# Attention with top-32 scores, then two feed-forward layers: the threshold from fours of scores, a stricter hand-over to GpSimd, shared work tiles, a new order of the steps

## The chip, the cores and the metric

One core of one Trainium2 chip. The metric is the device time of one execution in microseconds, the median of several runs.

## The reference

Attention over 4 batches, 8 heads, 576 positions and 64 dimensions, where each row keeps only the scores that reach its 32nd largest; then two feed-forward layers (512 to 2048 to 512) on the 2304 tokens, the first with a rational function between its products, the second with a squared relu.

```python
scores = scale * np.matmul(q, k.transpose(0, 1, 3, 2))
kth = np.partition(scores, -top_k, axis=-1)[..., -top_k:-top_k + 1]     # top_k = 32
scores = np.where(scores >= kth, scores, -1e9)
attn = np.exp(scores - max); attn = attn / (sum + 1e-9)
x = attn @ v                                                             # tokens x 512
h = x @ w_in;  g = P(h) / (Q(h) + 1e-6);  x = g @ w_out                  # P cubic, Q = 1 + |b0||h| + |b1|h2
h = x @ w_in2; x = np.maximum(h, 0) ** 2 @ w_out2
```

## The kernel before

The kernel is written as steps, and a planner written in Python sets the order of all instructions before anything runs.

**The steps.** `load_q`, `load_k` and `load_v` fetch and split operands into two fp16 halves. `attend(t, j)` (line 596) does one pair of heads for one of 18 tiles of 128 tokens: TensorE writes scores to `ps_sx`, ScalarE copies them to `sb`, VectorE finds the threshold, ScalarE takes the exponential to `ex`, VectorE masks it and sums it (`ex<-sb,kth,ex`), ScalarE and GpSimd split it into `ahl` (line 674), and SP issues a transposing DMA to `at`. The product with v (`mix`, line 684) comes three heads later (`LAGA`) and writes `xn`; after the last head the tile is transposed into `xT`. `w_load` fetches one of 32 weight units as 64-bit floats, makes them 32-bit on VectorE in `f4k` (lines 747 to 749) and splits them; 7 stay in SBUF (`wr`), 25 go back to DRAM (`wd`) and are reloaded into the ring `wt`. `consts1` and `consts2` need all units of their layer. The feed-forward works in ten blocks of 1 or 2 tiles; step u of a block computes the hidden product of unit u (`g1`), its function (`rational`, line 881, or `relu2`, line 905), and the output product of unit u - 2 (`g2`).

**The threshold before.** Scores i and i + 288 form a pair. VectorE writes the larger of each pair and the smaller of each, finds the 32 largest of the 288 larger ones (`largest`, line 632: MAX8 four times, MATCH_REPLACE8 three times) and the 8 largest of the smaller ones, and merges the two lists in `kths` and `kth` (lines 658, 659). `more` notes rows in which eight smaller ones would not do; if there is one, the whole kernel runs again with an exact search (line 1031).

**The order.** `at` (line 961) gives each step a place, read between knots of the list `KN`; a step comes no sooner than those it needs. The steps are sorted by place and each operation takes its step's place as its priority. `Plan.emit` then plays the engines with costs: an engine that is free takes the ready operation of the lowest place. `ANY` operations may go to GpSimd or VectorE; VectorE counts as `PEN` later. Instructions that GpSimd and VectorE can't run side by side (`port`: all of GpSimd's, and VectorE's with two inputs in SBUF) take turns in this play. In hardware nothing orders them except line 286: a GpSimd operation waits for the VectorE operation that held the port last, if it held it less than `LATE` = 500 ns earlier in the play:

```python
if e == "Pool" and holder is not None and holder.eng[0] == "DVE" and now < port + LATE:
    o.behind = holder
```

Each tile tag has a ring of `BUFS` places (line 472), given out in the order in which the steps name them. Each engine, and SP's DMA queue with it, runs its instructions in the order so planned.

Of the kernel before, what the change touches and what calls it, by code (L numbers as in the profile page):

```python
# [15 lines left out]
OP = mybir.AluOpType  # L16
# [9 lines left out]

PEN = 1e4

KN = [-1000000, 1000000000, 0, 34900, 89700, 131400, 186900, 217700, 292000, 325300, 345200, 429100,
# [5 lines left out]

LATE = 500.0
BEHIND = mybir.DependencyInfo(mybir.DependencyClass.Sync, mybir.DependencyReason.DATA)
# [19 lines left out]
class View:  # L57
# [42 lines left out]
    def bitcast(self, dt):  # L100
# [3 lines left out]
        return v  # L104

    def ap(self):
        t = self.tile
        if t.real is None:
            key = (t.tag, t.slot)
            if key not in t.pool[1]:  # L110
                name = f"{t.tag}_{t.slot}"
                t.pool[1][key] = t.pool[0].tile(list(t.shape), t.dtype, name=name, tag=name)
            t.real = t.pool[1][key]
        a = t.real
        for what, x in self.steps:
            if what == "get":
                a = a[x]
            elif what == "bitcast":
                a = a.bitcast(x)
            elif what == "pairs":  # L120
# [16 lines left out]
class Op:  # L137
    __slots__ = ("eng", "dur", "nbytes", "calls", "need", "next", "tiles", "prio", "ready", "n", "first", "start", "got", "port", "behind", "last")

# [10 lines left out]
class Plan:  # L150
# [4 lines left out]
    def __init__(self, tc):  # L155
        self.tc, self.ops, self.at, self.cur = tc, [], 0.0, None

# [25 lines left out]
    def _op(self, eng, cost, nbytes):  # L183
# [3 lines left out]
        o.nbytes, o.calls, o.need, o.next, o.tiles, o.prio, o.ready = nbytes, [], 0, {}, {}, self.at, 0.0  # L187
        o.n, o.first, o.port = len(self.ops), [], False
        self.ops.append(o)
# [20 lines left out]
    def emit(self):  # L210
# [19 lines left out]
        while events:  # L230
# [18 lines left out]
            for e in engines:  # L249
# [3 lines left out]
                while ready[e]:  # L253
# [187 lines left out]
def tile_topk_attention_moe_moe(ctx: ExitStack, tc: tile.TileContext, qx, kx, vx, vtx, vraw, wx, ma, mb, out):  # L441
# [25 lines left out]
    def run(exact):  # L467

        plan = Plan(tc)
        E = Engines(nc, plan)  # L470
        plan.at = KN[0] - 1e6
        BUFS = dict(ks=2, kacc=2, kf=2, ksc=2, ki=2, khn=2, kl=5, kd=5, vs=2, vh=5, vts=1, vt=5,
                    qs=1, qh=1, ql=1, qacc=2, qf=2, qsc=2, qi=2, qt=2, sc=2, nsc=2, top=2, w=1, kths=2, kth=2, bias=4, z=4, at=4, zi=5,
                    xn=2, xhl=2, xT=2, f4k=2, wt=6, sq=1, m_r=3, m_f=3, m_q=3, g1h=3, g1l=3, g2h=3, g2l=3,
                    yn2=2, yf=2, ysc=2, yis=4, yhl=1, yT=1, zd=2, zo=1, ps_sx=1, ps_h=2)
# [116 lines left out]
        waiting = []  # L592
        xns, kths_of, scs = {}, {}, {}
        more = new([P, NT, H], BF16, "more")

        def attend(t, j):
# [23 lines left out]
            for b, lo, hi in ps:  # L620

                whole = (b, H // 2 - 1) in kv if j == 0 else scs[t, b] 
                scs[t, b] = whole
                if j == 0 or not whole:
# [19 lines left out]
            else:  # L644

                if j == 0:
                    kths_of[t] = new([P, H, 9], F32, "kths"), new([P, H], F32, "kth")
                kths, kth = kths_of[t]
                h2 = slice(2 * j, 2 * j + 2)
                tb = tbs[pair % len(tbs)]  # L650
                E.tt("DVE", w[:, :, :S // 2], sb2[:, :, :S // 2], sb2[:, :, S // 2:S], OP.max)
                E.tt("DVE", w[:, :, S // 2:], sb2[:, :, :S // 2], sb2[:, :, S // 2:S], OP.min)
                for e in range(2):
                    big, small = w[:, e, :S // 2], w[:, e, S // 2:]
                    largest(top[:, e], big, big, K)
                    E.max8(tb[:, e, 1:], small)

                E.tt("DVE", kths[:, h2], top[:, :, K - 1:K - 10:-1], tb, OP.min)
                E.reduce(kth[:, h2], kths[:, h2], OP.max)
                kth = [kth[:, 2 * j + e:2 * j + e + 1] for e in range(2)]  # L660
                if j == H // 2 - 1:

                    E.tt("DVE", more[:, t], kths[:, :, 8], kths_of[t][1], OP.is_ge)
            z, zi = new([P, 2], F32, "z"), new([P, 2], F32, "zi")
# [46 lines left out]

        sbs, exs, ahls, tbs = [], [], [], []
        for n in range(2):
            tbs.append(new([P, 2, 9], F32, f"tb{n}"))
            E.memset("Pool", tbs[-1][:, :, 0], -NEG)
        for n in range(2):
# [17 lines left out]
        resident, scratch = {}, {}  # L734
        nres = [0]

        def w_load(m, u, io):
# [25 lines left out]
            if keep:  # L763
                wt = new([P, 2, 2, 512], F16, f"wr{nres[0]}")
                nres[0] += 1
            else:
                wt = new([P, 2, 2, 512], F16, "wt")
# [113 lines left out]
        def rational(hp, n, u):  # L881
# [75 lines left out]

        KVA = 4
# [6 lines left out]
        def between(ka, kb, f):  # L965
            return (ka, kb, f, KN[ka] + (KN[kb] - KN[ka]) * f)

        def item(n):
            t = min(max(n, 0) // H, NT - 1)
            return between(2 + t, 3 + t, n / H - t)  # L970

        def moe_at(m, i, k):

            a = 3 + NT + 2 * (m * NB + i)
            return between(a, a + 1, k / (NU + LAG))

        def w_at(m, k):
            a = 3 + NT + 4 * NB + 5 * m
            n = min(k // 4, 3)
            return between(a + n, a + n + 1, k / 4 - n)  # L980

        NK = 3 + NT + 4 * NB + 10
        start, end = (0, 0, 0.0, KN[0]), (1, 1, 0.0, KN[1])
        at(start, load_q, 0)
        at(start, load_k, 0, 0)
        first = (NK, NK, 0.0, KN[NK])
        scale = [at(first, v_scale)]
        seen = {(0, 0): [at(first, load_v, 0, 0, after=scale)]}
        items = []
        for n in range(NT * H):  # L990
            t, h = divmod(n, H)
            need = items[-1:]
            for b, _, _ in parts(t):
                j = h // 2
                if (b, j) not in seen:
                    seen[b, j] = [at(item(n - KVA), f, b, j, after=a) for f, a in ((load_k, ()), (load_v, scale))]
                need += seen[b, j]
            if h == 0 and t > 0:
                need.append(at(item(n - KVA), load_q, t))
            if h % 2 == 0:  # L1000
                items.append(at(item(n), attend, t, h // 2, after=need))
        items.append(at(item(NT * H), mix_rest, after=items[-1:]))
        ready = []
        for m in range(2):
            for k in range(2 * NU):
                ready.append(at(w_at(m, k), w_load, m, k // 2, k % 2))
            ready += scale
            ready = [at(w_at(m, 2 * NU), (consts1, consts2)[m], after=ready)]
            for i, (t0, n) in enumerate(blocks):
                x = min(((t0 + n) * H + LAGA - 1) // 2, NT * H // 2)  # L1010
                last = [items[x]] if m == 0 else [firsts[i]]
                for k, f in enumerate(moe_steps(m, i)):
                    last = [at(moe_at(m, i, k), f, after=last + ready)]
                if m == 0:
                    firsts[i] = last[0]
        for x, n, f in sorted(steps, key=lambda s: s[:2]):
            plan.at = x
            f()
        if not exact:
            plan.at = KN[1]  # L1020
            bad, n, flag = new([P, 1], F32, "bad"), new([P, 512], F32, "ps_h"), new([P, 1], I32, "flag")
# [57 lines left out]
```

## Time and profile before

| | |
|---|---|
| median of 3 runs | 1321.45 us (1319.78 to 1321.8) |
| the profiled execution's own time | 1320.17 us |
| its span, first to last instruction | 1318.4 us |
| mean granted TensorE clock in the span | 0.940 |

The profile is of one execution. Its names are PE (TensorE), PEld (TensorE's weight loads), DVE (VectorE), ACT (ScalarE), POOL (GpSimd) and SP with its DMA queue SPq. Tiles carry the names of the code without their buffer numbers, and L362 is the helper line through which almost every operation of VectorE, ScalarE and GpSimd is recorded, so groups are told apart by tile. "Mean ns" is the duration of one instruction from start to end; neighbours on one engine can overlap, so busy time is less than count times mean.

### The profile page before, as it was taken

The page shows a single profiled execution, that of the slowest core. Times are in us where ns is not written, and L with a number is a line of the kernel's source. Part 1 is how long each engine was busy: PE and PEld are TensorE (multiplying, and loading weights), DVE is VectorE, ACT ScalarE, POOL GpSimd, SP SyncE. Part 2 cuts the span into 40 slices and gives each one's busy share as a digit, 9 for nine tenths or more (in the row PEclk, how much of TensorE's full clock was granted, in tenths as well). Part 3 has the DMA queues.
Part 4 walks back from the last instruction along what each step waited for, and adds up shares of the span by engine and source line. Part 5 has one row for each costly group of instructions (what it writes and reads, how often), then busy time and mean ns, then how long its engine had stood idle before and what let it go on. Part 6 is the DMA issues. An engine that isn't in the chain of part 4 may idle for free. (4 is left out here: it accounts for less than half of the span.)

```text
span 1318.4 us, 25413 instructions
## 1 busy us (share of the span) xinstructions
PE 1045.2 (79%) x8808; PEld 673.3 (51%) x8808; DVE 1129.3 (86%) x3298; ACT 997.3 (76%) x1796; POOL 553.4 (42%) x458
## 2 busy tenths in 40 slices
PE   2123254555789698979996999999999899999998
PEld 1112132333456365646653666656665566666665
DVE  5999989879999999999989899998999999983511
ACT  7866667667878787879987789888887877775543
POOL 2234424234454445445655555654653564330000
PEclk9999995665889998989998999999999999999999
DMA  8977775878579675778886768879777877865854
GB/s 259 288 250 232 224 245 177 252 222 241 161 187 258 178 184 161 198 171 211 222 198 161 186 179 207 235 168 215 193 197 177 197 191 171 206 195 175 251 183 161
DMA packets 299868, 269.18 MB, mean 204 GB/s; under 512 B 236368, under 2 KB 246096, under 8 KB 299728
## 3 DMA queue, kind: packets, MB, share of 16 engines
q1 hardware_dynamic: 299728, 267.45, 75.1%
q8 instruction: 71, 1.16, 0.4%
q14 instruction: 69, 0.57, 0.1%
HBM read 183.50 MB, written 17.83 MB: 153 GB/s over the span
## 5 line engine op out<-in xcount | busy, mean ns | idle before, releaser
L428 PEld LDWEIGHTS <-wt 128*128 128x128 f16 x3120 | 286.4, 101 | 65.2 <-issue 8.8
L362 POOL TENSOR_TENSOR ahl<-ex,ahl 128x576 f16<-128x576 f32 x144 | 182.5, 1282 | 300.0 <-ACT ahl L362 113.7
L362 DVE MAX8 top<-w 128x8 f32<-128x288 f32 x576 | 239.4, 444 | 0.1
L428 PE MATMUL ps_h<-xT,wt 128*128 128x256 f16 (+1 forms) x1680 | 193.4, 273 | 5.5 <-ACT f4k L362 2.1
L362 DVE MATCH_REPLACE8 w<-top,w 128x288 f32<-128x288 f32 x432 | 188.3, 440 | 0.0
L428 PE MATMUL ps_h<-yT,wt 128*128 128x256 f16 (+1 forms) x1440 | 159.0, 263 | 0.0
L428 PE MATMUL ps_sx<-vh,at 128*128 128x64 f16 (+1 forms) x1920 | 88.7, 202 | 81.7 <-DMA at<-ahl 58.9
L428 PEld LDWEIGHTS <-at 128*128 128x128 f16 (+1 forms) x2400 | 96.3, 107 | 111.7 <-DMA at<-ahl 74.5
L428 PE MATMUL ps_y<-wt,g1h 128*128 128x512 f16 x432 | 137.3, 401 | 13.0 <-DMA wt<-wd 9.7
L428 PE MATMUL ps_y<-wt,g2h 128*128 128x512 f16 x432 | 129.0, 380 | 0.0
L362 ACT ACTIVATE ex<-sb,bias,sc 128x576 f32<-128x576 f32 x144 | 119.1, 861 | 10.7 <-POOL ahl L362 7.4
L362 DVE TENSOR_TENSOR w<-sb 128x576 f32<-128x576 f32 x144 | 108.3, 768 | 19.1 <-ACT sb L362 18.8
L362 POOL TENSOR_TENSOR m_f<-m_f,m_q 128x512 f32<-128x512 f32 (+1 forms) x55 | 67.8, 1233 | 133.8 <-ACT m_q L362 63.5
L362 ACT ACTIVATE sb<-ps_sx 128x576 f32<-128x576 f32 x144 | 92.5, 642 | 40.0 <-PE ps_sx L428 39.6
L362 DVE SCALAR_TENSOR_TENSOR ex<-sb,kth,ex 128x577 f32<-128x577 f32 x144 | 119.0, 858 | 1.3 <-ACT sq L362 0.6
L428 PEld LDWEIGHTS <-qt 64*128 64x128 f16 (+3 forms) x640 | 41.2, 100 | 132.6 <-issue 108.0
L428 PE MATMUL ps_sx<-kl,qt 64*128 64x512 f16 (+1 forms) x320 | 74.5, 317 | 40.7 <-ACT xn L362 22.2
L362 ACT ACTIVATE ahl<-ex 128x576 f16<-128x576 f32 x144 | 93.2, 674 | 8.8 <-DVE ex L362 8.6
L362 ACT ACTIVATE xn<-ps_sx,zi 128x64 f32<-128x64 f32 x144 | 44.2, 307 | 72.1 <-PE ps_sx L428 71.4
L362 POOL TENSOR_TENSOR wt<-f4k,wt 128x1024 f16<-128x1024 f32 x25 | 53.2, 2129 | 108.1 <-ACT ahl L362 36.8
L428 PE MATMUL ps_y<-wt,g1l 128*128 128x512 f16 x216 | 86.6, 401 | 7.4 <-POOL g1l L362 7.4
L362 ACT ACTIVATE f4k<-ps_h,cu 128x512 f32<-128x512 f32 (+1 forms) x80 | 50.8, 636 | 48.0 <-PE ps_h L428 48.0
(164 smaller groups left out, 2357.5 us busy)
## 6 DMA issues: line engine op xcount, KB each, us to landing
wt<-wd SPq DMA_DIRECT2D x250, 512.0 KB, 4.1
wt<-in_wx_dram SPq DMA_DIRECT2D x64, 512.0 KB, 5.9
wd<-wt SPq DMA_DIRECT2D x25, 512.0 KB, 3.1
qs<-in_qx_dram SPq DMA_DIRECT2D x18, 256.0 KB, 4.3
ks<-in_kx_dram SPq DMA_DIRECT2D x16, 288.0 KB, 4.2
wt<-in_vraw_dram SPq DMA_DIRECT2D x12, 384.0 KB, 6.2
kd<-khn SPq DMA_DIRECT2D x64, 72.0 KB, 3.1
out_dram<-zo SPq DMA_DIRECT2D x18, 256.0 KB, 2.5
```

Source lines behind the costliest of these rows:

```text
L362: return f(**{k: self.ap(x) for k, x in kw.items()})
L428: self.plan.add("PE", self.cols(out) * passes / 2.4 + 3, lambda e: self.nc.tensor.matmul(self.ap(out), self.ap(lhsT), self.ap(rhs), start= ...
```

## The change

1. The threshold search goes by fours. The larger of each pair are paired once more: `u` holds the 144 largest of fours. The 8 largest of each of three remaining groups (two halves of the smaller ones of the second pairing, 72 scores each, and the 288 smaller ones of the first) are written behind them, and the 32 largest are sought among these 168. `kths`, `kth` and `tb` go; `more` compares each group's 8th with the threshold, now once a pair of heads.
2. GpSimd waits for VectorE's last holder of the port however long ago that was in the play.
3. The rational step's `m_f` and `m_q` become two halves of one `f4k` tile, of which there are 5 instead of 2. Its first two activations change places, and its second and third VectorE operations with them.
4. Every step has a place of its own in a list `PLACES` of 358 numbers, in place of 72 knots; the needs between the first loads are written out; `PEN` is 8457 instead of 10000.

```diff
-PEN = 1e4
-KN = [-1000000, 1000000000, 0, 34900, 89700, 131400, 186900, 217700, 292000, 325300, 345200, 429100,
...
-LATE = 500.0
+PEN = 8457
+PLACES = [-101131, -104946, -1423, 566, -464, -4302, -788, 916, -725, -1069, 1322, 1333, -1127, 780, 1067, 2727, 4109,
...
+          141508, 141328, 141417, 144751, 141347, 138173, 140740]
...
-                        if e == "Pool" and holder is not None and holder.eng[0] == "DVE" and now < port + LATE:
+                        if e == "Pool" and holder is not None and holder.eng[0] == "DVE":
                             o.behind = holder
...
-                    xn=2, xhl=2, xT=2, f4k=2, wt=6, sq=1, m_r=3, m_f=3, m_q=3, g1h=3, g1l=3, g2h=3, g2l=3,
+                    xn=2, xhl=2, xT=2, f4k=5, wt=6, sq=1, m_r=3, g1h=3, g1l=3, g2h=3, g2l=3,
...
-                E.tt("DVE", w[:, :, :S // 2], sb2[:, :, :S // 2], sb2[:, :, S // 2:S], OP.max)
-                E.tt("DVE", w[:, :, S // 2:], sb2[:, :, :S // 2], sb2[:, :, S // 2:S], OP.min)
+                h2, n = slice(2 * j, 2 * j + 2), S // 4
+                u = new([P, 2, n + 24], F32, "u")
+                E.tt("DVE", w[:, :, :2 * n], sb2[:, :, :2 * n], sb2[:, :, 2 * n:S], OP.max)
+                E.tt("DVE", w[:, :, 2 * n:], sb2[:, :, :2 * n], sb2[:, :, 2 * n:S], OP.min)
+                E.tt("DVE", u[:, :, :n], w[:, :, :n], w[:, :, n:2 * n], OP.max)
+                E.tt("DVE", w[:, :, :n], w[:, :, :n], w[:, :, n:2 * n], OP.min)
                 for e in range(2):
-                    big, small = w[:, e, :S // 2], w[:, e, S // 2:]
-                    largest(top[:, e], big, big, K)
-                    E.max8(tb[:, e, 1:], small)
-
-                E.tt("DVE", kths[:, h2], top[:, :, K - 1:K - 10:-1], tb, OP.min)
-                E.reduce(kth[:, h2], kths[:, h2], OP.max)
-                kth = [kth[:, 2 * j + e:2 * j + e + 1] for e in range(2)]
-                if j == H // 2 - 1:
-
-                    E.tt("DVE", more[:, t], kths[:, :, 8], kths_of[t][1], OP.is_ge)
+                    for k, (lo, hi) in enumerate(((0, n // 2), (n // 2, n), (2 * n, 4 * n))):
+                        E.max8(u[:, e, n + 8 * k:n + 8 * k + 8], w[:, e, lo:hi])
+                    largest(top[:, e], u[:, e], w[:, e, :n + 24], K)
+                kth = [top[:, e, K - 1:K] for e in range(2)]
+
+                E.tt("DVE", more[:, t, h2], u[:, :, n + 7::8], top[:, :, K - 1:K].wide(3), OP.is_ge)
...
-            f, q, r, gh, gl = (t(x, F16 if x[0] == "g" else F32) for x in ("m_f", "m_q", "m_r", "g1h", "g1l"))
-
+            fq = new([P, 2, 512], F32, "f4k")
+            f, q = fq[:, 0, :n], fq[:, 1, :n]
+            r, gh, gl = (t(x, F16 if x[0] == "g" else F32) for x in ("m_r", "g1h", "g1l"))
+
+            E.act(f, hp, AF.Identity, scale=k("f_s"), bias=k("f_b"))
             E.act(q, hp, AF.Abs, scale=k("q_s"))
-            E.act(f, hp, AF.Identity, scale=k("f_s"), bias=k("f_b"))
+            E.tt("DVE", f, f, hp, OP.mult)
             E.stt(q, q, k("bd"), hp, OP.add, OP.mult)
-            E.tt("DVE", f, f, hp, OP.mult)
...
-        def at(x, f, *args, after=()):
-            steps.append((max([x[3]] + [steps[k][0] for k in after]), len(steps), lambda: f(*args)))
+        def at(f, *args, after=()):
+            p = 10.0 * PLACES[len(steps)]
+            steps.append((max([p] + [steps[k][0] for k in after]), len(steps), lambda: f(*args)))
             return len(steps) - 1
```

`wide(3)` repeats a column three times as an operand.

## Rows read from the trace of the kernel before

**Rows 1.** Page, part 1: busy us (share of the span) xinstructions, by engine.
```profile
PE 1045.2 (79%) x8808; PEld 673.3 (51%) x8808; DVE 1129.3 (86%) x3298; ACT 997.3 (76%) x1796; POOL 553.4 (42%) x458
```

**Rows 2.** Windows by stage: length, busy us (x) by engine, clock, DMA share, GB/s.
```profile
0.00:300.00 300.00, 112.80 (x806) 72.60 (x806) 260.85 (x774) 209.99 (x350) 101.28 (x82) 0.87 0.78 236
300.00:1150.00 850.00, 770.31 (x6692) 490.77 (x6693) 798.23 (x2388) 693.10 (x1270) 437.00 (x365) 0.95 0.78 195
1150.00:1318.40 168.40, 162.12 (x1312) 109.92 (x1310) 70.18 (x137) 94.20 (x177) 15.13 (x13) 0.99 0.61 192
```

**Rows 3.** Critical chain, some of its pieces: start us, us, what.
```profile
1114.65 5.55 DMA xT<-xhl
...
1147.58 2.62 PE ps_h L428 x24
...
1309.11 3.27 PE ps_y L428 x15
```

**Rows 4.** Timeline at 640 us, VectorE, then GpSimd: start us, us, instruction.
```profile
640.33 1.86 DVE L362 SCALAR_TENSOR_TENSOR ex<-sb,kth,ex 128x577 f32<-128x577 f32 x1
...
640.30 1.28 POOL L362 TENSOR_TENSOR g1h<-m_f,m_r 128x512 f16<-128x512 f32 x1
```

**Rows 5.** By tile, VectorE, whole span: ns min/median/max, first and last start us.
```profile
L362 DVE TENSOR_TENSOR w<-sb x144: 726/747/1482, 19.0 to 1137.9; 128x576 f32<-128x576 f32 x144
...
L362 DVE SCALAR_TENSOR_TENSOR ex<-sb,kth,ex x144: 800/812/1859, 28.2 to 1147.6; 128x577 f32<-128x577 f32 x144
...
L362 DVE TENSOR_TENSOR kths<-top,tb x72: 158/170/1251, 27.3 to 1145.3; 128x18 f32<-128x18 f32 x72
...
L362 DVE SCALAR_TENSOR_TENSOR m_q<-m_q,cc,g1h x80: 471/742/1752, 186.5 to 1247.2; 128x512 f32<-128x512 f32 x64, 128x256 f32<-128x256 f32 x16
```

**Rows 6.** Groups on VectorE, 300 to 1150 us: busy us, mean ns, idle before.
```profile
L362 DVE MAX8 top<-w 128x8 f32<-128x288 f32 x479 | 198.6, 444 | 0.0
...
L362 DVE SCALAR_TENSOR_TENSOR ex<-sb,kth,ex 128x577 f32<-128x577 f32 x120 | 98.8, 858 | 0.2
L362 DVE TENSOR_TENSOR w<-sb 128x576 f32<-128x576 f32 x118 | 89.3, 772 | 15.8 <-ACT sb L362 15.5
...
L362 DVE SCALAR_TENSOR_TENSOR m_q<-m_q,cc,g1h 128x512 f32<-128x512 f32 x56 | 45.4, 811 | 1.5 <-POOL g1h L362 1.3
...
L362 DVE TENSOR_TENSOR kths<-top,tb 128x18 f32<-128x18 f32 x60 | 17.4, 290 | 0.2
...
L362 DVE TENSOR_TENSOR g1l<-m_f,m_r 128x512 f16<-128x512 f32 x14 | 9.5, 678 | 0.0
...
L362 DVE TENSOR_TENSOR g1h<-m_f,m_r 128x512 f16<-128x512 f32 x8 | 5.6, 701 | 2.5 <-ACT m_r L362 1.3 <-ACT m_f L362 1.1
```

**Rows 7.** Timeline inside one search, VectorE, then GpSimd.
```profile
613.98 0.81 DVE L362 MAX8 top<-w 128x8 f32<-128x288 f32 x2
614.71 0.08 DVE L362 MATCH_VALUE_LOAD w<-top,w 128x8 f32 x1
614.77 0.45 DVE L362 MATCH_REPLACE8 w<-top,w 128x288 f32<-128x288 f32 x1
...
613.05 2.53 POOL L362 TENSOR_TENSOR ahl<-ex,ahl 128x576 f16<-128x576 f32 x2 [3.31 <-ACT ahl L362]
```

**Rows 8.** Groups on VectorE over the whole span, by shape.
```profile
L362 DVE TENSOR_TENSOR m_f<-m_f,ps_h 128x512 f32<-128x512 f32 x64 | 43.3, 677 | 3.5 <-ACT m_f L362 3.5
...
L362 DVE TENSOR_TENSOR m_f<-m_f,ps_h 128x256 f32<-128x256 f32 x16 | 6.6, 413 | 0.2 <-ACT m_f L362 0.2
```

**Rows 9.** Windows: the 100 us from 600 us on, columns as in rows 2.
```profile
600.00:700.00 100.00, 96.32 (x816) 63.07 (x814) 94.44 (x277) 90.43 (x168) 60.21 (x53) 0.98 0.84 218
```

**Rows 10.** Waits: TensorE 300 to 1150 us, SP's queue whole span: us, times, longest.
```profile
PE ps_sx L428 <- DMA at<-ahl: 32.1, 21, 5.6
...
PE ps_y L428 <- POOL g1l L362: 9.7, 5, 6.1
...
SPq L436 <- POOL ahl L362: 169.1, 64, 9.7
```

More of the change, by code (lines that the diff above doesn't have):

```diff
@@ L104, in bitcast, with wide @@
         return v
+    def wide(self, n):
+        return self._with(self.shape[:-1] + (n,), self.box, ("wide", n))
     def ap(self):
@@ L119, in ap @@
                 a = a.bitcast(x)
+            elif what == "wide":
+                a = bass.AP(a.tensor, a.offset, list(a.ap)[:-1] + [[0, x]])
             elif what == "pairs":
@@ L137 @@
 class Op:
-    __slots__ = ("eng", "dur", "nbytes", "calls", "need", "next", "tiles", "prio", "ready", "n", "first", "start", "got", "port", "behind", "last")
+    __slots__ = ("eng", "dur", "nbytes", "calls", "need", "next", "tiles", "prio", "ready", "n", "first", "start", "got", "port", "behind", "last", "step")
 LATENCY = {"ACT": (145.0, {"PE": 163.0, "Pool": 170.0}), "DVE": (128.0, {"Pool": 155.0}), "PE": (197.0, {"PE": 0.0}),
@@ L155, in __init__ @@
     def __init__(self, tc):
-        self.tc, self.ops, self.at, self.cur = tc, [], 0.0, None
+        self.tc, self.ops, self.at, self.cur, self.step = tc, [], 0.0, None, -1
     def tile(self, pool, shape, dtype, tag, bufs=1):
@@ L187, in _op @@
         o.nbytes, o.calls, o.need, o.next, o.tiles, o.prio, o.ready = nbytes, [], 0, {}, {}, self.at, 0.0
-        o.n, o.first, o.port = len(self.ops), [], False
+        o.n, o.first, o.port, o.step = len(self.ops), [], False, self.step
         self.ops.append(o)
@@ L470, in run @@
         E = Engines(nc, plan)
-        plan.at = KN[0] - 1e6
+        plan.at = FIRST - 1e6
         BUFS = dict(ks=2, kacc=2, kf=2, ksc=2, ki=2, khn=2, kl=5, kd=5, vs=2, vh=5, vts=1, vt=5,
-                    qs=1, qh=1, ql=1, qacc=2, qf=2, qsc=2, qi=2, qt=2, sc=2, nsc=2, top=2, w=1, kths=2, kth=2, bias=4, z=4, at=4, zi=5,
-                    xn=2, xhl=2, xT=2, f4k=2, wt=6, sq=1, m_r=3, m_f=3, m_q=3, g1h=3, g1l=3, g2h=3, g2l=3,
+                    qs=1, qh=1, ql=1, qacc=2, qf=2, qsc=2, qi=2, qt=2, sc=2, nsc=2, top=2, w=1, u=1, bias=4, z=4, at=4, zi=5,
+                    xn=2, xhl=2, xT=2, f4k=5, wt=6, sq=1, m_r=3, g1h=3, g1l=3, g2h=3, g2l=3,
                     yn2=2, yf=2, ysc=2, yis=4, yhl=1, yT=1, zd=2, zo=1, ps_sx=1, ps_h=2)
@@ L592, in run @@
         waiting = []
-        xns, kths_of, scs = {}, {}, {}
-        more = new([P, NT, H], BF16, "more")
+        xns, scs = {}, {}
+        more = new([P, NT, H, 3], BF16, "more")
         def attend(t, j):
@@ L620, in attend @@
             for b, lo, hi in ps:
-                whole = (b, H // 2 - 1) in kv if j == 0 else scs[t, b]
-                scs[t, b] = whole
+                whole = t > b * S // P
                 if j == 0 or not whole:
@@ L644, in attend @@
             else:
[L646 to L650, printed above, removed]
-                E.tt("DVE", w[:, :, :S // 2], sb2[:, :, :S // 2], sb2[:, :, S // 2:S], OP.max)
-                E.tt("DVE", w[:, :, S // 2:], sb2[:, :, :S // 2], sb2[:, :, S // 2:S], OP.min)
-                for e in range(2):
-                    big, small = w[:, e, :S // 2], w[:, e, S // 2:]
-                    largest(top[:, e], big, big, K)
-                    E.max8(tb[:, e, 1:], small)
-                E.tt("DVE", kths[:, h2], top[:, :, K - 1:K - 10:-1], tb, OP.min)
-                E.reduce(kth[:, h2], kths[:, h2], OP.max)
-                kth = [kth[:, 2 * j + e:2 * j + e + 1] for e in range(2)]
-                if j == H // 2 - 1:
-                    E.tt("DVE", more[:, t], kths[:, :, 8], kths_of[t][1], OP.is_ge)
+                h2, n = slice(2 * j, 2 * j + 2), S // 4
[4 more added lines that the diff above has]
+                E.tt("DVE", w[:, :, :n], w[:, :, :n], w[:, :, n:2 * n], OP.min)
+                for e in range(2):
+                    for k, (lo, hi) in enumerate(((0, n // 2), (n // 2, n), (2 * n, 4 * n))):
[3 more added lines that the diff above has]
+                E.tt("DVE", more[:, t, h2], u[:, :, n + 7::8], top[:, :, K - 1:K].wide(3), OP.is_ge)
             z, zi = new([P, 2], F32, "z"), new([P, 2], F32, "zi")
@@ L709, in mix @@
                 E.dma_transpose(xT[i][:, :, k * P:(k + 1) * P], xhl.flat(), 2 * P * 1024)
[L712 to L715, printed above, removed]
+        sbs, exs, ahls = [], [], []
         for n in range(2):
@@ L734, in run @@
         resident, scratch = {}, {}
-        nres = [0]
         def w_load(m, u, io):
@@ L763, in w_load @@
             if keep:
-                wt = new([P, 2, 2, 512], F16, f"wr{nres[0]}")
-                nres[0] += 1
+                wt = new([P, 2, 2, 512], F16, f"wr{(n * RESIDENT) // (4 * NU)}")
             else:
@@ L955, in moe_steps @@
             return [lambda u=u: step(u) for u in range(NU + LAG)]
-        KVA = 4
         steps, firsts = [], {}
-        def at(x, f, *args, after=()):
-            steps.append((max([x[3]] + [steps[k][0] for k in after]), len(steps), lambda: f(*args)))
+        def at(f, *args, after=()):
+            p = 10.0 * PLACES[len(steps)]
+            steps.append((max([p] + [steps[k][0] for k in after]), len(steps), lambda: f(*args)))
             return len(steps) - 1
[L965 to L988, printed above, removed]
+        q0 = at(load_q, 0)
+        k0 = at(load_k, 0, 0)
+        scale = [at(v_scale)]
+        seen = {(0, 0): [k0, at(load_v, 0, 0, after=[k0] + scale)]}
         items = []
@@ L995, in run @@
                 if (b, j) not in seen:
-                    seen[b, j] = [at(item(n - KVA), f, b, j, after=a) for f, a in ((load_k, ()), (load_v, scale))]
+                    seen[b, j] = [at(load_k, b, j, after=seen[b, 0][:1] if j else ())]
+                    seen[b, j].append(at(load_v, b, j, after=seen[b, j] + scale))
                 need += seen[b, j]
+            if t == 0:
+                need = need + [q0]
             if h == 0 and t > 0:
-                need.append(at(item(n - KVA), load_q, t))
+                need.append(at(load_q, t))
             if h % 2 == 0:
-                items.append(at(item(n), attend, t, h // 2, after=need))
-        items.append(at(item(NT * H), mix_rest, after=items[-1:]))
+                items.append(at(attend, t, h // 2, after=need))
+        items.append(at(mix_rest, after=items[-1:]))
         ready = []
@@ L1005, in run @@
             for k in range(2 * NU):
-                ready.append(at(w_at(m, k), w_load, m, k // 2, k % 2))
+                ready.append(at(w_load, m, k // 2, k % 2))
             ready += scale
-            ready = [at(w_at(m, 2 * NU), (consts1, consts2)[m], after=ready)]
+            ready = [at((consts1, consts2)[m], after=ready)]
             for i, (t0, n) in enumerate(blocks):
@@ L1012, in run @@
                 for k, f in enumerate(moe_steps(m, i)):
-                    last = [at(moe_at(m, i, k), f, after=last + ready)]
+                    last = [at(f, after=last + ready)]
                 if m == 0:
@@ L1016, in run @@
         for x, n, f in sorted(steps, key=lambda s: s[:2]):
-            plan.at = x
+            plan.at, plan.step = x, n
             f()
+        plan.step = -2
         if not exact:
-            plan.at = KN[1]
+            plan.at = LAST
             bad, n, flag = new([P, 1], F32, "bad"), new([P, 512], F32, "ps_h"), new([P, 1], I32, "flag")
```

1 line of the change is left out of this document (added), and 27 rows, old and new, of tables (KN, PLACES).

## The prediction, made before the changed kernel ran

> **What bounds the kernel now.** I read the engine totals first [rows 1]. VectorE leads with 86% of the span, but that is an average over unlike stages, so the second view cuts the span into three [rows 2]. Up to 300 us the weights, q, k and v come in and TensorE works 113 us of 300. From 300 to 1150 us VectorE is busy 798.23 of 850 us (94%) and TensorE 770.31 (91%). From 1150 us on TensorE is busy 162 of 168 us and VectorE 70. The chain of waits begins, as far as it was followed, at 1114.65 us with the transposed tokens of a feed-forward block, and ends in output products at 1309.11 us [rows 3]. The reader is to see a relay: VectorE sets when the last attention tile is through, then TensorE works off two blocks of the first layer and three of the second, which by the sorted places all come behind that tile or hang on the block ahead of it. So a microsecond saved on VectorE before 1150 us moves the tail forward by a microsecond, if TensorE and the port can follow; saved later it is worth nothing.
>
> A second bound hides behind VectorE. The diff's "port" is the thing that GpSimd and two-input VectorE instructions hold in turns. In [rows 4] GpSimd ran g1h from 640.30 us for 1.28 us, and VectorE's masking product, started 0.03 us later, took 1.86 us where its median is 0.812 [rows 5]: it stood until GpSimd was done. Over 300 to 1150 us GpSimd holds the port 437.0 us [rows 2]; on VectorE the masking product holds it 98.8, the pairwise max and min 89.3, the product with g1h 45.4, the compare for kths 17.4 and three smaller groups 21.9 [rows 6]. Together 710 of 850 us: the port is taken 84% of the time.
>
> **The threshold search: the working time.** Rows give durations, but VectorE's instructions overlap: two MAX8 in a row last 0.81 us, not 2 x 0.444 [rows 6], and starts in a run are about 0.08 us closer than the durations [rows 7]. So a MAX8 over 288 advances the engine by 0.365 us, a MATCH_REPLACE8 with its value load by 0.36 + 0.065, a max or min over 576, by its median of 0.747 [rows 5], by 0.665. No row has the new sizes. The 512 and 256 wide forms of one multiply give 677 - 413 ns for 256 elements, 1.03 ns each [rows 8]; with this slope, a MAX8 over 168 advances by 0.24, over 72 by 0.14, a MATCH_REPLACE8 over 168 by 0.235 (+0.065), a max or min over 288 by 0.365.
> Before, per pair of heads: 2 x 0.665, then per head 5 x 0.365 + 3 x 0.425 = 3.10, then 0.19 for kths, kth and the share of the flag compare: 7.72 us. After: 2 x 0.665 + 2 x 0.365, then per head 2 x 0.14 + 0.365 + 4 x 0.24 + 3 x 0.30 = 2.51, then 0.08 for the flag compare: 7.16 us. The saving is 0.56 us a pair, 40 us over 72 pairs: 34 us of it in the 60 pairs from 300 to 1150 us, 6 in the 12 before. Bounds: if nothing overlapped and every instruction cost its whole duration, 9.38 against 9.19, or 14 us in all (five instructions more per pair eat the rest); if an instruction had no fixed part, 816 elements less a pair, 61 us. I take 40, since the starts in the rows are what the engine does.
>
> The Trainium skill has a rule against this change: "VectorE: DVE Perf Modes", section "The DRAIN you can't avoid", says that the next instruction does not start until the pipeline is empty, so small ones pay in full. By that rule the saving would be the 14 us above. The trace differs here: the starts 613.98, 614.71 and 614.77 leave no such gap.
>
> **The search: the port.** MAX8 and MATCH_REPLACE8 have one input, and GpSimd runs beside them: two GpSimd operations from 613.05 to 615.58 us lie inside one search [rows 7]. The change takes 85 us of that cover away (6.20 less 5.02 us a pair) and adds two two-input operations: 0.73 + 0.08 us a pair, less kths. From 300 to 1150 us the port then needs 710 + 49 - 17 = 741 us, VectorE 798 - 34 = 764. Three operations of a first-layer step and one of a second-layer step may run on either engine; one moved to VectorE frees the port by 1.28 [rows 4] less 0.60 us (g1l's 678 ns [rows 6] less the overlap) and costs VectorE 0.60. If the port can be filled to 92% (100 us from 600 on come near: GpSimd 60.2 there, plus the middle's 32 of VectorE [rows 9]) nothing need move and the stretch takes 764/0.94 = 813 us, 37 less. If it stays at 84%, some 50 products move, VectorE has 794 us of work, and the stretch takes 846, 4 less. Between these far ends I take a fill of 88%: 21 products moved, 826 us, **24 us less**. What is late next is GpSimd, then the transposes.
>
> **The first 300 us.** 12 pairs save 6 us; the DMA share is 0.78 and VectorE 87% busy [rows 2]. I take 5, bounds 0 and 6.
>
> **GpSimd always waits.** Before, its instruction waits for VectorE's last holder only if the plan has less than 500 ns between them; now always. What is queued behind the waiting instruction is GpSimd's own line: ahl, then transposes on SP (169.1 us of SP's waits are for ahl already [rows 10]), behind these the weight reloads, and then the products with v on TensorE, which lose 32.1 us to those transposes in the middle stretch [rows 10]. What it can win is collisions: mean less median, times the count from 300 to 1150 us, is 3.0 us for the pairwise max and min, 5.5 for the masking product, 7.2 for kths, 3.9 for the g1h product [rows 5, 6]; 20 us in all. Some of these are VectorE arriving while GpSimd works rightly, which no wait here mends. Gain 0 to 20, loss 0 to 32; I take 5 gained, by kths, which GpSimd's early starts hit most and whose result the mask no longer waits for.
>
> **Shared tiles and order.** The two work tiles of the rational step now share the ring of five with the weights and the second layer. SBUF stays the same and each step finds three places as before if the other users hold two; 0. Cover: TensorE has two buffers of scores ahead of it; without that, a step waits for one group of products, 1.3 us [rows 3]. In the rational step the two first activations swap, so the multiply by h can start one activation earlier and the other product one later: 0. The order: by the places, sorted, the first layer's first step still follows all 16 weights of that layer, now behind attention 2,0 instead of 1,1 and behind eight weights of the second layer instead of one. Seven loads moved ahead are 14 transfers in and up to 7 out on SP's queue, 42 unpacking instructions on VectorE and 7 subtractions on GpSimd, all moved and none added. The first layer starts later, where TensorE works 113 of 300 us [rows 2]; that sets nothing, as long as block 0 is through before block 1 needs TensorE. Last come, before and after, the same five blocks. I price order at 0, with 20 us either way: half a block of one layer, 4 units of 24 products of 2.62 us and 12 of 0.218 [rows 3].
>
> **Sum.** Against the profiled execution's 1320.17 us: 24 + 5 + 5 = 34 less, 1286. The median of the runs shown stands 1.3 higher: **1287 us**.
>
> **Rivals.**
> 1. The port takes it back: the fill stays at 84%, products move to VectorE, GpSimd is idle as often as now. For: the port is the only resource whose work grows, and it passes between engines more often. Against: [rows 9]. 1321 - 4 - 3 = 1314; at a little lower fill it is no change. 0.14.
> 2. Small instructions cost their full length. The 14 us instead of 40: about 1308. Against: the starts in [rows 7]. 0.07. The page named above would have it so.
> 3. Slower: GpSimd, held behind a late VectorE instruction, sends ahl late, SP's transposes stand at the head of its queue, and TensorE, in order, stands at the products with v with feed-forward products behind. If the 32.1 us at transposes and the 9.7 at g1l [rows 10] double, and VectorE's gain goes unused because the tiles reach their blocks late, it is 1321 + 42 - 30 = 1333. It decides once TensorE loses over 34 us more between 300 and 1150 us, where it now has 80 us idle [rows 2]. For: GpSimd then has 30 us less free port. Against: three heads lie between a search and its product. 0.11.
> 4. The order does more than I can price: VectorE's idle 52 us in the middle shrink and tail work is done earlier, under 1252. 0.04.
> 5. The change doesn't hold: were eight scores of one lower group above a row's threshold, the exact kernel would run behind, another 1300 us. On the reference's inputs the counted maximum is seven in 18432 rows: 0.01.
>
> **The numbers.** The forecast has 0.63. The range 1252 to 1322 holds it with rivals 1 and 2; its low end is 40 + 20 + 9 us below the median, its high end no change. A measurement of this kernel can tell about 0.2% (2.6 us) from no change. Faster is the forecast, rivals 2 and 4 and two thirds of rival 1: 0.83; same the rest of that: 0.05; slower rivals 3 and 5: 0.12.
>
> **What would show it.** MAX8 over 168 near 320 ns and over 72 near 220; VectorE's work down by 40 us plus moved products at 0.6 each; last search near 1105 instead of 1137.9 us [rows 5]; a tail still near 168 us; fewer long masking products. Wrong, if the last search comes earlier but the tail grows (TensorE), if VectorE's share of g1h, m_f and g1l grows by over 50 (port), or if waits for at<-ahl double.

## The result and the profile after

The changed kernel takes 1308.85 us (median of 4 runs, 1305.48 to 1309.71) against 1321.39: ratio 0.9903, 95% interval 0.9883 to 0.9922. The gain is 12.6 us; the forecast was 34. The profiled execution took 1305.48 us.

Page, part 1, of the changed kernel [rows 1]:

```profile
PE 1037.6 (80%) x8808; PEld 670.3 (51%) x8808; DVE 1110.5 (85%) x3655; ACT 998.9 (77%) x1796; POOL 533.2 (41%) x441
```

Its windows by stage, columns as in [rows 2]; the last one runs past the end of the span:

```profile
0.00:300.00 300.00, 110.14 (x834) 70.69 (x835) 270.93 (x875) 219.60 (x366) 100.05 (x77) 0.92 0.83 246
300.00:1150.00 850.00, 779.92 (x6802) 500.84 (x6800) 783.49 (x2667) 697.60 (x1278) 422.60 (x353) 0.96 0.79 196
1150.00:1400.00 250.00, 147.54 (x1179) 98.75 (x1177) 56.07 (x115) 81.67 (x156) 10.59 (x11) 0.99 0.36 116
```

VectorE works 18.8 us less (1129.3 to 1110.5), not 40. GpSimd does 17 instructions fewer. At 1150 us TensorE has 1179 matmuls left, before it had 1312, and both tails run at 7.7 to 7.8 matmuls a microsecond: the 133 matmuls are 17 us, so the whole gain is there by 1150 us. The mean granted TensorE clock of the span rose from 0.940 to 0.958. The groups of VectorE, by shape (busy us, mean ns | idle before):

```profile
L386 DVE MAX8 top<-w 128x8 f32<-128x168 f32 x432 | 121.7, 322 | 0.1
...
L386 DVE MATCH_REPLACE8 w<-top,w 128x168 f32<-128x168 f32 x288 | 89.4, 318 | 0.0
...
L386 DVE TENSOR_TENSOR w<-w 128x288 f32<-128x288 f32 x72 | 54.4, 755 | 0.0
...
L386 DVE MAX8 u<-w 128x8 f32<-128x72 f32 x288 | 45.7, 218 | 0.1
...
L386 DVE TENSOR_TENSOR u<-w 128x288 f32<-128x288 f32 x72 | 32.5, 452 | 0.0
...
L386 DVE TENSOR_TENSOR more<-u,top 128x6 bf16<-128x6 f32 x72 | 21.7, 301 | 0.6
```

The one-input sizes cost what was worked out (322, 318 and 218 ns; 320, 316 and 221 from the durations before and the slope of 1.03 ns). Of the two new two-input operations the max (u) lasts 452 ns, the min (w<-w), of the same shape, 755. The timeline shows why, VectorE, then GpSimd:

```profile
651.92 0.45 DVE L386 TENSOR_TENSOR u<-w 128x288 f32<-128x288 f32 x1
652.28 0.81 DVE L386 MAX8 u<-w 128x8 f32<-128x288 f32 x2
653.02 1.08 DVE L386 TENSOR_TENSOR w<-w 128x288 f32<-128x288 f32 x1
...
652.50 1.28 POOL L386 TENSOR_TENSOR ahl<-ex,ahl 128x576 f16<-128x576 f32 x1 [4.43 <-DVE u L386]
```

GpSimd is released by the max and takes the port for 1.28 us; the min starts 0.52 us later and ends at 654.10 us, 0.32 us after GpSimd: it stands until GpSimd is through and does most of its work then. Over 72 pairs that is 72 x (755 - 452) = 22 us. (The Trainium skill, "SBUF — State Buffer", section "Who interferes with whom", calls the port an exclusive lock; the trace agrees, the min is done only 0.32 us after GpSimd's record has ended.)

So the first reading was: the search saves 40 us, 22 are lost at the port, the relay hands on the rest. The experiments took this apart. Ratios below are against the kernel before, run on the same chip.

### The profile page after: what moved, and what is told of

It is laid out like the page before. It is cut to its first block, busy times and chain, and to the rows that moved or that the text cites. A ratio compares the mean times of both kernels' runs of the same rounds, so it can differ in the third digit from the quotient of the medians.

```text
span 1303.7 us, 25763 instructions
## 1 busy us (share of the span) xinstructions
PE 1037.6 (80%) x8808; PEld 670.3 (51%) x8808; DVE 1110.5 (85%) x3655; ACT 998.9 (77%) x1796; POOL 533.2 (41%) x441
## 4 chain that ended last, share of the span: by engine, by line
PE 44%; DVE 22%; ACT 15%; DMA 10%; issue 5%; POOL 2%; SPq 1%; ACTq 0%; POOLq 0%; DVEq 0%
PE ps_h L452 19%; PE ps_y L452 18%; PE ps_sx L452 8%; DVE f4k L386 7%; DMA at<-ahl 6%; DVE w L386 5%; ACT f4k L386 4%; DVE top L386 2%; DVE ex L386 2%; DVE u L386 2%; ACT sq L386 2%; ACT ex L386 2%; ACT ahl L386 1%; ACT m_r L386 1%; ACT sb L386 1%
## 5 line engine op out<-in xcount | busy, mean ns | idle before, releaser
L386 POOL TENSOR_TENSOR ahl<-ex,ahl 128x576 f16<-128x576 f32 x144 | 183.3, 1283 | 391.0 <-DVE u L386 105.4
L452 PE MATMUL ps_y<-wt,g1h 128*128 128x512 f16 x432 | 132.8, 390 | 6.1 <-DVE g1h L386 3.2
L386 DVE MAX8 top<-w 128x8 f32<-128x168 f32 x432 | 121.7, 322 | 0.1
L386 DVE SCALAR_TENSOR_TENSOR ex<-sb,top,ex 128x577 f32<-128x577 f32 x144 | 114.9, 821 | 2.0 <-ACT ex L386 1.8
L386 ACT ACTIVATE f4k<-f4k 128x512 f32<-128x512 f32 (+1 forms) x160 | 92.5, 583 | 26.7 <-DVE f4k L386 24.7
L386 DVE MAX8 u<-w 128x8 f32<-128x72 f32 (+1 forms) x432 | 104.6, 295 | 0.1
L386 POOL TENSOR_TENSOR f4k<-f4k 128x512 f32<-128x512 f32 (+1 forms) x44 | 53.8, 1223 | 113.8 <-DVE f4k L386 81.3
L386 POOL TENSOR_TENSOR g1h<-f4k,m_r 128x512 f16<-128x512 f32 (+1 forms) x60 | 73.1, 1220 | 56.7 <-ACT m_r L386 31.0
L386 DVE MATCH_REPLACE8 w<-top,w 128x168 f32<-128x168 f32 x288 | 89.4, 318 | 0.0
```

The source lines that it names most:

```text
L386: return f(**{k: self.ap(x) for k, x in kw.items()})
L452: self.plan.add("PE", self.cols(out) * passes / 2.4 + 3, lambda e: self.nc.tensor.matmul(self.ap(out), self.ap(lhsT), self.ap(rhs), start= ...
```

## Experiments

**1. The min right behind the max**, nothing else moved. In each pair of `mates`, `a` is the max and `b` the min.

```diff
+        for a, b in self.mates:
+            order.remove(b)
+            order.insert(order.index(a) + 1, b)
+            for o in order:
+                if o.behind is a:
+                    o.behind = b
```

> The changed kernel with one thing moved: in VectorE's order the second-level min (w<-w) stands right behind the second-level max (u<-w), and the GpSimd operations that waited for the max wait for the min. All other instructions keep their order. Theory (the missing gain is VectorE standing at the port: w<-w means 755 ns against 449 when alone, 22 us over 72 pairs): w<-w falls to a mean under 470 ns, VectorE's busy time falls by about 20 us, the time falls to 1285 to 1297 us. Rival (the port was full anyway, so GpSimd's 0.4 us later starts push the same time elsewhere): w<-w gets short, the other long records grow, the time stays within 1303 to 1312.

Measured 1312.7 us, 0.9926 (0.9903 to 0.9949), which can't be told from the changed kernel. The standing goes from this operation and turns up at others: VectorE's busy time stays, 1112.0 us against 1110.5. Its groups in that run:

```profile
L393 DVE SCALAR_TENSOR_TENSOR f4k<-f4k,cc,g1h 128x512 f32<-128x512 f32 x64 | 51.8, 810 | 2.0 <-POOL g1h L393 1.7
...
L393 DVE TENSOR_TENSOR w<-w 128x288 f32<-128x288 f32 x72 | 33.0, 458 | 2.5
...
L393 DVE TENSOR_TENSOR g1l<-f4k,m_r 128x512 f16<-128x512 f32 x23 | 17.5, 764 | 1.8 <-POOL f4k L393 1.4
```

So 21 us of long min records gave no time. But VectorE's standing as a whole did not shrink here, only its place changed; what less standing is worth, this run can't say. The run `pool_less` of experiment 5 can: with shorter GpSimd operations the min's mean is 564 ns and VectorE's busy time falls by 21.6 us, with no work of its own taken away:

```profile
PE 1040.9 (80%) x8808; PEld 672.9 (52%) x8808; DVE 1088.9 (84%) x3655; ACT 998.1 (77%) x1796; POOL 456.0 (35%) x441
```

Its gain is 5.9 us, GpSimd's own 77 us included. The first reading falls by that.

**2. The same by the planner**, and with it a new plan (max and min become one operation, which holds the port).

```diff
+                with plan.group("DVE"):
                     E.tt("DVE", u[:, :, :n], ..., OP.max)
                     E.tt("DVE", w[:, :, :n], ..., OP.min)
```

> The changed kernel with second-level max and min planned as one operation of VectorE, so that the planner itself puts nothing between them, and re-plans all the rest. Theory (standing at the port): as in the run that only moves the min, 1280 to 1300 us, with w<-w under 470 ns. Rival (places fitted to the old durations; any re-planning costs what the fit had gained): 1305 to 1325 us.

1356.19 us, 1.0263 (1.0237 to 1.029), with w<-w at 458 ns: slower than either expectation, though no operation was added or dropped. The new plan does move 42 operations from GpSimd to VectorE (441 to 399 instructions on GpSimd).

**3. One part at a time.** The search alone in the kernel before:

> The kernel before with the new threshold search alone (old places, old rule of waiting, old work tiles). Theory (the search is worth 40 us of work less some 22 us of standing at the port, the other parts about nothing): 1300 to 1310 us. Rival (the search gains nothing net and the new order brings the 12 us): 1318 to 1326 us. Second rival (the other parts cost what the search lost): under 1297 us.

1318.39 us, 0.9966 (0.9946 to 0.9986): 4.5 us. This too is a new plan, since the search's durations changed: 30 operations that either engine may do moved from GpSimd to VectorE, and VectorE's busy time fell only from 1129.3 to 1123.9 us. The changed kernel with the old search:

> The changed kernel with the old threshold search (the other three parts stay). Theory (parts two to four are worth about nothing): 1316 to 1328 us. Rival (the order, the waiting rule and the tiles bring the gain): 1305 to 1314 us. Second rival (they cost): over 1330 us.

1377.24 us, 1.041 (1.0381 to 1.0439). With the old order (knots, needs of the first loads and PEN of before):

> The changed kernel with the old order of the steps and the old PEN; new search, stricter wait and shared tiles stay. Theory (the search alone with old places gave 1318 against 1321, so the rest of the 12 us is the order): 1314 to 1330 us. Rival (the shared tiles or the wait brought it): 1304 to 1312 us.

1338.89 us, 1.0136 (1.0115 to 1.0157). With tiles of their own for m_f and m_q:

> The changed kernel with m_f and m_q in tiles of their own again and f4k in two places; search, wait, places and PEN stay. It is re-planned by that. Theory (places fit one plan): 1320 to 1350 us. Rival (the rings hardly bind, so the plan hardly changes): 1304 to 1314 us.

1336.7 us, 1.0119 (1.0093 to 1.0146). With the 500 ns limit back, which leaves the plan alone:

```diff
-                        if e == "Pool" and holder is not None and holder.eng[0] == "DVE":
+                        if e == "Pool" and holder is not None and holder.eng[0] == "DVE" and now < port + 500.0:
```

> The changed kernel with the 500 ns limit on GpSimd's wait put back; every engine's instructions and their order stay as they are, only waits go. Theory (the stricter wait neither gains nor costs much: GpSimd is held in order by its own late inputs anyway): within 3 us of the changed kernel's 1308.85. Rival (it was a loss, GpSimd held behind VectorE): 1295 to 1304 us. Second rival (it keeps GpSimd from starting ahead of VectorE and so keeps collisions away): 1313 to 1325 us, with more long VectorE records.

1311.54 us, 0.9909 (0.9883 to 0.9935): nothing that can be told from the changed kernel. So three of the four parts, taken out, cost far more than the change gains, and the fourth is neutral. But the three runs are new plans as well, and each price is that of a part and of a plan together. Gains of parts don't add here. The new order alone in the kernel before was not run.

**4. Is it the re-planning?** PEN alone, in the changed kernel and in the one before:

```diff
-PEN = 8457
+PEN = 1e4
```

> The changed kernel with PEN back at 10000 instead of 8457: no instruction changes, but the plan is played anew and engines get other orders. Theory (the 358 places fit one plan; any other plan of the same work loses what they gained): 1318 to 1350 us. Rival (the two re-planned runs lost time by their own contents, not by being re-planned): 1304 to 1313 us.

> The kernel before with PEN at 8457 instead of 10000: no instruction changes, only the plan is played anew. Theory (any plan but the one that the places were fitted to is slower): 1326 to 1350 us. Rival (the knots of before are coarse and forgiving, only the 358 single places are brittle): 1314 to 1326 us.

1339.45 us, 1.0121 (1.0101 to 1.0142), and 1332.29 us, 1.0089 (1.007 to 1.0107). No operation is added or dropped in either (9 and 26 move from GpSimd to VectorE), and by the ratios 29 and 12 us go. The window from 300 to 1150 us and the rest, of the changed kernel with PEN back:

```profile
300.00:1150.00 850.00, 767.34 (x6574) 491.15 (x6574) 770.44 (x2611) 675.51 (x1233) 396.48 (x332) 0.94 0.76 189
1150.00:1500.00 350.00, 173.65 (x1410) 117.15 (x1409) 80.37 (x182) 105.82 (x201) 23.21 (x21) 0.99 0.33 100
```

and of the changed kernel with the old search:

```profile
300.00:1150.00 850.00, 734.93 (x6249) 470.54 (x6250) 762.97 (x2270) 650.78 (x1184) 366.98 (x307) 0.91 0.72 181
1150.00:1500.00 350.00, 214.34 (x1745) 142.34 (x1743) 113.69 (x262) 132.72 (x246) 35.29 (x31) 0.99 0.42 121
```

All engines are busy less in the middle than in the changed kernel, and TensorE has more left at 1150 us: 1179 matmuls in the changed kernel, 1312 before, 1410 and 1745 here. That says where the time of these plans lies, not why: behind 1150 us TensorE works nearly without a break, so what is left then is the time still to come.

**5. What is a microsecond of each engine worth?** Work taken from one engine, planned as if it were there, so that all orders stay (the kernels leave that part of the result out). First on the kernel before, where the prediction's relay can be tried itself.

```diff
-                    E.max8(tb[:, e, 1:], small)
+                    E.max8(tb[:, e, 1:], small[:, :72], plan=small)
```

> The kernel before with one-input VectorE work taken away and nothing else: the MAX8 over the smaller scores reads 72 of 288 (216 a row are left out there), planned as before, orders unchanged. 32 us less, all of it in searches. The prediction's own step (VectorE sets when the last attention tile is through, and a microsecond saved there moves the tail by one): 1287 to 1297 us. Theory now (the fixed order's chain passes through all engines, VectorE's 94% is not the bound): 2 to 8 us, 1313 to 1320.

1320.02 us, 1.0005 (0.9985 to 1.0025). VectorE's busy time in the middle fell from 798.23 to 775.82 us and the time did not move. Windows and the MAX8 of that run:

```profile
300.00:1150.00 850.00, 772.04 (x6722) 493.32 (x6723) 775.82 (x2388) 697.20 (x1275) 440.38 (x367) 0.95 0.78 196
```

```profile
L362 DVE MAX8 tb<-w 128x8 f32<-128x72 f32 x144 | 31.3, 217 | 0.0
```

TensorE in the kernel before:

```diff
+                        if m == 0 and 1 <= i <= 5:
+                            plan.cur.dur = (plan.cur.dur[0] + (512 / 2.4 + 3),)
+                        else:
                             E.mm(y, gh[:, s], wt[:, c, 1], False, False)
```

> The kernel before with TensorE work taken away and nothing else: in blocks 1 to 5 of the first layer the product of g's high half with the weights' low half is left out, planned as before, orders unchanged. 35 us less between about 330 and 880 us. The prediction's step (TensorE has room before the last tile): under 3 us, 1318 to 1323. Theory now (TensorE holds the largest part of the chain): 6 to 15 us, 1306 to 1316, more than VectorE's cut gives.

1313.82 us, 0.9947 (0.9918 to 0.9976): 7 us. TensorE is short of time where I took it to have room. The same in the changed kernel, and the other engines:

> The changed kernel with one-input VectorE work taken away and nothing else: the MAX8 over the 288 smaller scores reads only 72 of them (216 scores a row are left out of that group), planned as if it read all, so all orders stay. That is 144 x 0.225 = 32 us less of work that does not hold the port. Theory now (port and VectorE share the bound: what VectorE saves beside GpSimd it spends standing at the port later): it gains under half, 1293 to 1306 us. Rival (VectorE's working time is the bound): 1275 to 1285 us. Second rival (neither, the order and TensorE set the time): within 3 us of 1308.85.

> The changed kernel with one-input VectorE work added and nothing else: the MAX8 over the 288 smaller scores is done twice, the second planned at no cost, so all orders stay. 144 x 0.365 = 53 us more. It is the cut turned round: what were 53 us longer searches to cost in this order? If the search's saved working time carries the gain: 40 to 55 us more, 1349 to 1364. Theory now (a searched microsecond is worth about a tenth to a third either way, the rest hides): 1312 to 1328 us.

> The changed kernel with port time taken from GpSimd and nothing else: it computes only half of the columns of ahl's low part (288 of 576 are left out), planned as before, so all orders stay. 144 x 0.62 = 89 us less of port time, no VectorE work changed. Theory now (the port is a bound beside VectorE): VectorE's long records go (overlap 55 us falls under 25) and the time falls by 20 to 45 us, 1264 to 1289. Rival (VectorE's and TensorE's own work set the time, the port only looks busy): 0 to 8 us, 1300 to 1309.

> The changed kernel with ScalarE work taken away and nothing else: only half of the columns of ahl's high part are written (288 of 576 are left out), planned as before, so all orders stay. 144 x 0.24 = 35 us less of ScalarE. Theory (TensorE's stream sets the time): 0 to 8 us gained, 1300 to 1309. Rival (ScalarE, between scores and everything else, is the bound): 1275 to 1290.

> The changed kernel with TensorE work taken away and nothing else: in blocks 1 to 5 of the first feed-forward layer the product of g's high half with the weights' low half is left out, planned as before, so all orders stay. 5 blocks x 32 matmuls of 0.216 us = 35 us less, all of it between about 320 and 870 us, none in the tail. Theory now (TensorE's stream, in its fixed order, sets the time from 350 us on; VectorE's and GpSimd's busy shares mislead): 1280 to 1292 us, at least half of the 35. Rival (no one engine sets it, each hides behind the others): as with VectorE, under 5 us, 1303 to 1310.

| work in the changed kernel (as planned) | ratio (95%) | against 0.9903 |
|---|---|---|
| VectorE, 32 us less | 0.9876 (0.9855 to 0.9897) | 3.6 us less |
| VectorE, 53 us more | 0.9977 (0.9957 to 0.9998) | 9.8 us more |
| GpSimd, 79 us less (89 were meant) | 0.9858 (0.9836 to 0.9879) | 5.9 us less |
| ScalarE, 35 us less | 0.9888 (0.9859 to 0.9917) | 2.0 us less |
| TensorE, 35 us less | 0.9835 (0.9816 to 0.9855) | 9.0 us less |

(The last column is the difference of the ratios times 1321; the changed kernel's own interval is 0.9883 to 0.9922, so VectorE's cut and ScalarE's can't be told from nothing.) Per microsecond: TensorE 0.26, VectorE 0.11 to 0.18, GpSimd 0.07, ScalarE 0.06. TensorE's 9 us lie between what was expected of it (half of the 35) and its rival (under 5).

TensorE's value may be too low. Its busy time fell by 21.6 us, not 35, and the granted clock fell with the cut, from 0.958 to 0.945 in the profiled executions; the other runs agree (0.945 to 0.951 against 0.954 to 0.958), and in the kernel before it fell from 0.940 to 0.922. The engine totals of the run with TensorE's cut:

```profile
PE 1016.0 (78%) x8648; PEld 660.4 (51%) x8648; DVE 1110.5 (85%) x3655; ACT 998.9 (77%) x1796; POOL 533.5 (41%) x441
```

Per microsecond of busy time that went or came, by such totals, it is TensorE 0.42, VectorE 0.14 (25.5 us less) to 0.24 (40.8 us more), GpSimd 0.08 and ScalarE 0.07: the same order. GpSimd's ahl in its run (`pool_less`), 731 instead of 1283 ns, 144 times:

```profile
L386 POOL TENSOR_TENSOR ahl<-ex,ahl 128x288 f16<-128x288 f32 x144 | 104.1, 731 | 428.2 <-DVE u L386 120.0 <-ACT ahl L386 73.8 <-ACT xn L386 45.9
```

Do VectorE and the port cover for each other, or do all four?

> The changed kernel with both of the earlier cuts, 32 us less of one-input VectorE work and 89 us less of GpSimd's port time, in the unchanged order. Theory (TensorE's stream sets the time): about the sum of the two alone, 1295 to 1304 us. Rival (port and VectorE bound it together, so that each cut alone is caught by the other): far more than the sum, 1265 to 1285 us.

1297.82 us, 0.9849 (0.9825 to 0.9872): 7.1 us, where the two alone make 9.5. They don't cover for each other: that rival had asked for 1265 to 1285.

> The changed kernel with the four cuts at once (32 us of VectorE, 89 of GpSimd, 35 of ScalarE, 35 of TensorE), orders unchanged. The cuts alone gave about 3.5, 6, 2 and 9 us. If the chain passes from engine to engine and each cut is worth the share of the chain that its engine holds: about the sum, 1282 to 1294 us. If each cut is caught by the other engines: far more than the sum, 1255 to 1278 us. If transfers and the wait for them fill the chain: less than the sum, 1294 to 1302 us.

1283.88 us, 0.9725 (0.971 to 0.974): 23.5 us, where the four alone make 20.5. Within their intervals the shares add up. The rest of some 180 us taken away is hidden in this order. The chain of waits from 300 to 1150 us of the changed kernel agrees in rank, share of the window by line:

```profile
by line: PE ps_h L452 19.1%; PE ps_y L452 18.2%; PE ps_sx L452 10.9%; DMA at<-ahl 8.6%; ACT f4k L386 5.1%; issue 4.9%; DVE f4k L386 4.1%; DVE w L386 3.6%; ACT ex L386 2.6%; DVE ex L386 1.9%; ACT m_r L386 1.8%; DVE u L386 1.7%; ACT ahl L386 
```

TensorE has 48%, VectorE's search some 5% (w and u in this row; the row ends before the smaller lines). The sizes don't agree: TensorE's 48% stands against the 0.26 or 0.42 above. And up to 300 us the chain is another one; by the page it holds over the whole span:

```profile
PE 44%; DVE 22%; ACT 15%; DMA 10%; issue 5%; POOL 2%; SPq 1%; ACTq 0%; POOLq 0%; DVEq 0%
```

In the kernel before, the chain could be followed only from 1114.65 us on [rows 3].

## Why the prediction was wrong

The direction held; the size was 2.7 times too large. Of the 34 us, 29 (24 and 5) rest on the relay, the other 5 on GpSimd's wait. The kernel got faster, but mostly not in the way that was forecast, so the right direction is in part luck. Step by step:

- **The relay failed.** "So a microsecond saved on VectorE before 1150 us moves the tail forward by a microsecond, if TensorE and the port can follow": on the kernel before, 32 us saved moved it by nothing (1.0005, at most some 2 us by the interval). Its second half holds, the end follows the last search at the same distance (below); its first half fails, VectorE's work does not set when that search comes. In the profiled execution with 32 us less it started at 1133.7 us instead of 1137.9, and that execution was itself 3.6 us faster than its run's median. I read the bound from a busy share of 94% while the chain, which would have tested it, was not there before 1114 us. In the changed kernel's order a searched microsecond is worth 0.18 by the 53 us that were added and 0.11 by those cut: 40 us of search are worth 4 to 7 us there, and the search alone, in a plan of its own, gave 4.5. This is the step that made 34 out of it.
- **The working time** held for one-input operations. The second max and min and the flag compare, all two-input, were put at 0.81 us a pair with the overlap taken off; as records they are 452 + 755 + 301 ns. The min's 22 us at the port were not in the sum; moved elsewhere (experiment 1) they gave no time, and with 21.6 us of standing really gone (`pool_less`) the gain was 5.9 us.
- **The port** as second bound (fill of 84, 88 or 92%) was a price for something that does not set the time: 79 us less of GpSimd gave 5.9 us. The 84% itself was not clean: the records it adds up hold VectorE's standing a second time (some 20 us by the prediction's own excess over the medians), and it leaves out two-input groups of about the same sum (g2l, f4k, vh, kl, vt and more, some 22 us); the two errors nearly cancel.
- **GpSimd always waits**: 5 us gained was put down, none found (0.9909 against 0.9903). Long records went where kths and the masking product stood (the latter's mean over the whole span fell from 858 to 821 ns) and came back at the min and at more (median 161 ns, mean 301).
- **Order and shared tiles at 0, with 20 us either way**, was wrong: the old order in place of the new one costs 31 us with the rest of the change, own tiles 29. Both are new plans, so what is shown is that parts and plan hang together: none of the new plans of the changed kernel that were tried came within 25 us of it. The gain itself, TensorE's 133 matmuls fewer at 1150 us, is not divided among the parts by these runs. What in the new order puts TensorE ahead stays open; the lead is not built at one place (by windows from the start it is 28 matmuls at 300 us, 81 at 600, 186 at 850). Nor is it told apart how much of the gain goes with the higher granted clock; the run with VectorE work added had 0.956 too and took 1317.58 us, so the clock alone does not bring it.
- **The tail** held: 180 us from the last search to the end before (1137.9 to 1318.4), 178 after (1126.0 to 1303.7, by the rows at the end). But the last search came at 1126.0, where the prediction had asked for about 1105.

Of the rivals, the first (products move to VectorE) is seen in small: 10 of the movable products (116 on VectorE before, 126 after), and 24 more than before in the run of the search alone. The second, short instructions at full length, had about 1308 us, next to the 1308.85 measured. That is luck: four MAX8 of 72 columns last 0.62 us together in the changed kernel, where one lasts 0.218, so they do overlap. None of the prediction's three signs of being wrong showed either: the tail did not grow, 10 products moved and not over 50 us of them, and TensorE's waits for at<-ahl fell from 32.1 to 23.1 us. It had no sign for a VectorE that is busy without setting the time. A cut of transfers was not tried; at<-ahl has 8.6% of the chain above.

## What to carry to other kernels

A high busy share was no bound here, in a kernel whose order is planned: before pricing an engine's saving, ask the chain of waits inside the stretch, or cut that engine's work with the order kept and see what it is worth. Where a planner with fitted priorities sets the order, a change of one duration or one weight re-plans everything, and the re-planning (12 to 48 us in the runs whose operations stayed the same) can be larger than the edit; a part's worth can then be measured only with the order held. And test an undone part with the plan held still, or the result is the plan's.

## What was not expected of the hardware

Two-input VectorE operations and GpSimd's take turns to the full: a min of 460 ns by its median took up to 1.93 us behind a GpSimd operation of 2.12 us. Taking such standing away at one place (21 us of records) changed nothing in the time, since VectorE then stood elsewhere.

The tile rows of the changed kernel, ns min/median/max, first and last start us (for the tail and for the min's longest record):

```profile
L386 DVE TENSOR_TENSOR w<-sb x144: 730/751/2612, 22.6 to 1126.0; 128x576 f32<-128x576 f32 x144
L386 DVE TENSOR_TENSOR w<-w x72: 440/460/1933, 27.3 to 1131.9; 128x288 f32<-128x288 f32 x72
```
